# Infini-attention beside an MLP: memory read as two 64-row products, VectorE with at most one SBUF operand, and another job order

## The chip, the cores and the metric

The kernel runs on one core of a Trainium2 chip. A core has TensorE (PE in the profile; its weight loads are PEld), VectorE (DVE), ScalarE (ACT), GpSimd (POOL) and SyncE (SP, which here issues most DMAs). SBUF is the working memory of 128 partitions; PSUM has eight banks of 128 x 512 f32, into which TensorE writes. The metric is device time in microseconds; before the change it is 690.04, the median of 3 runs (689.83 to 690.31).

## What is computed

x has 2048 rows of 512. It is normalised, then two branches are added to it:

```python
x = A_x
xn = _layernorm(x, axis=-1)
return x + _A_ref(xn, A_wq, A_wk, A_wv, A_wo, A_beta) + _B_ref(xn, B_w1, B_b1, B_w2, B_b2)
```

Branch B is an MLP of width 1792 with its own layer norm and GELU. Branch A is attention with 32 heads of 16 in four segments of 512 rows, with a compressed memory M, z carried from segment to segment:

```python
for s in range(N):
    qs, ks, vs = q[:, :, s], k[:, :, s], v[:, :, s]
    logits = jnp.einsum("bhqd,bhkd->bhqk", qs, ks) * scale + mask
    p = _softmax(logits, axis=-1)
    a_dot = jnp.einsum("bhqk,bhkd->bhqd", p, vs)
    pq = phi(qs)                      # where(t > 0, t + 1, exp(t))
    num = jnp.einsum("bhld,bhde->bhle", pq, M)
    den = jnp.einsum("bhld,bhd->bhl", pq, z)[..., None] + 1e-6
    a_mem = num / den
    o = g * a_mem + (1.0 - g) * a_dot
    pk = phi(ks)
    M = M + jnp.einsum("bhld,bhle->bhde", pk, vs)
    z = z + jnp.einsum("bhld->bhd", pk)
```

## The kernel before

Attention runs in 16 blocks i = 4 s + g: segment s, group g of eight heads (128 partitions of head dimensions). Large products are f16 in three terms: every operand is split into a high and a low half. For a block, `qk_proj` projects q and k into a PSUM bank, ACT writes the high half and, where phi is needed (q from segment 1 on, k up to segment 2), Exp of the bank into SBUF; `qk_low` forms the low half on DVE and sends both through DRAM (kd, qd) into the layout in which the scores are formed (kst, qst). `qk_phi` finishes phi on DVE: a minimum and a product in SBUF (L632), then a maximum of the bank plus that (L634, L638).

`m_job` forms scores a first time (L740) and reduces their masked maximum on DVE (L747); `m_row` turns the maxima to rows, which go through DRAM (md) into two further rows of qst. `s_job` forms the scores transposed with the maximum already subtracted (L782), ACT exponentiates them (L789), POOL clears the upper triangle (`s_mask`), `pv` multiplies with the values (L816, four column quarters of the array), and `o_norm` divides by the sum: Ln and Exp(-) on ACT, one Newton step on DVE (L662, L663), products on POOL.

The memory is read in `a_mem` for blocks 4 to 15. `z_cols` lays M and z out with zeros between heads (mx, on DVE). Four products of 128 rows give, for 128 tokens each, numerators and denominators with tokens on partitions (L681, two banks); DVE forms the reciprocal and the quotient (rd, L684 to L689, into rc); `a_turn` transposes it back with four transposes (L696) and ACT copies it to ame (L698), which `o_norm` adds on POOL.

The MLP is `d_job` (hidden tiles, L586 on w1s), `gelu` and `h_split` on ACT and POOL, and `e_jobs` (L931); `out_jobs` is the output projection (L951). Weights are scaled by powers of two from sums of squares: `w_trace` takes sums on TensorE with a reduction on DVE (L384), `w_scale` adds them over partitions with a product with ones (L414).

The order is written out: `ORDER` names, character by character, the stream from which the next job comes, and `BANKS` the PSUM bank of every `dense()`. Each engine takes its instructions in that order. A bank is written again when its readers are done. SP takes its DMAs in the same order.

Of the kernel before, what the change touches and what calls it, by code (L numbers as in the profile page):

```python
# [19 lines left out]
P = 128  # L20
# [5 lines left out]
H = 32  # L26
# [33 lines left out]
def streams():  # L60
# [78 lines left out]
    "auhhwhhhlkhhkhhbth6xc6khldlhhie$hfhhhhkjhx6f78$hhahhv$rg7%%8%k8%h8bR8cs8mRde8i&ff9m9gj9n&!n&#y&z((CA)9*(CD+(+2"  # L139
    "BBDo)(X*+X,)-,*(()X!*3oXX,9,XXYFZFF0Py1F.zpF,-o!FR4F#.Z-0FB9,.14BR4QFZF041/XZA,X/01/-/.4F$=4/=p:4E4P24#F2;F:=="  # L140
    "44:4G4GFGX=GF<XHGFF3>4HaI>::IHI>IFGqGb3Xc?X2GH;GFyFFdzG@XHf>XF:EHYCX<X?DiQZ0IIA>;IB1I>GJG<3KGXCLBe:XGG;ZHD@MPX"
    "4HNFFIIHQIO0IFFG1Z4f4<GGX?0@41GHHqFZFy0FGY>F4a[1?4zXjAFHFZIIIIb4@0B4414Z[[FEcJ4KXXd4440[1eBXfGGGZ4LXXFMG440G]F"
    "1FH4fUN4ZP^H0X1YFFFyH4OFFIIIZiAIGzF044444GFGCF]GGX4_ETX1H]H4Q]HIIIDIGJGKBGZH4LPVX0BaXy1ZzG0GFMC4X1H4AZ4^FID0H_"
    "NOIITIFG4XGFUG4H4G1GFHBH4XFFIIIIFFJYFKURR4B4FLFMbFZNFRXOE0S4W4GcFGeX4144HGGGRF5HFIIHQIIdFFGSZG5FHFPyG0GGXzSFH1"
    "Z2VHASIIQIEI0GJGKLGXC13BX2DPfUXTGMGW444fNZV44H0HHjIIIOQIBFFG41a4bGGX4iHGGF3Y44H4HFFF4yFZ5FI01IIzBZAI0F1JZFX04X"
    "C4K1DZ404FjXX1B44X4EXX4YT4Z44LFG2cG4M44eGFiFd01X43H4FGGZN0HXXFF5IHIIOIGFGXXGGF2XWFG1FZfHf0XPVHFU4441Z01YZyE44H"
    "a3zIIIQIGGJ44UK4L4C4AGGMTG4D4N4WH4bPHHOIIIIGGGXB0BVXGGFyFF1HzHHBFIcIdAIZIRCFFFe01RDXFJKFFXZi0RLMXXFWTN41fR4fE4"
    "GZGGB4440XHOG1FGH4SHFFFIIYIQISGGa5FVZ4X4GG0UFXP4HH2FG1Z0FbyH4FzFIQIIAI1S5XSPBFZJ4X03KLCc1EZDM4GiGT5NOG4XBXGGj4"
    "H4W0HH4IQIII1GGF444FGG4VXGFFyHHHFFFIYIII24dZ4e440F13zFZ0FJ4XC4D1Z0XXFEfXK41BTABXL4Z4XM44041GGGPX44UGFFH44HNU4f"
    "4OFYZGF04WXV44XH1F2ZFIIIIFGFy53G0zFFXX1XGHZGG44FHC440TXXXIED1QYI2HZI0IGG41JKH4BZjj44GGGH34L4UBMX4HWNXX0OIIIIFF"  # L150
    "G4144FZG0FyF1ZGH0zFXXGF1G4Z4XFH0FFHYIIIIVCUBFRJ4KREDL1M4WNT4ORGBGGS5Z240GFHFS4FF1GRFF5HHFIZIIIGG0y1FFF4zHSVF4C"
    "4Z40GGG4HDE44HSIITIIG5G1J44XXK4ZLGGBMBGHXXXNXH4HFI3I2IOI0GGHF3441WVyzGFG4XGFFHCY4FFF444HXIZT0I1Z20IB1DIFFJ4ZXX"
    "04KX1BFLZX40E1X4XY4ZM0NF1FZG4444GF5UG4XH0414GGFXH4FFHIIZOI2IGFF440X1GGFHXZ40G1GHF34HXFXXYEIIZII01ZJW444KGG44LV"
    "GG34GMHH4H444IINOI0IGG1HG44G4GZ4W440HH41IIII4Z04JKL1444M444N4O44SSSS5555"
# [4 lines left out]
    "01234567012345670123460123647013654701542670546173250641732570641257106457106457103645120365412306524306512430"  # L159
    "65713062451372046130472610342561037425036714023674012743610273406217306723146723156042713560421630541263045126"  # L160
    "30452630451263745126345126347152630471526045271352671532467135246357021463570214635721426357426357421063574210"
    "63547231506472361507236175236415273641503641752034172053724105637120357612035712036571203471206514270651427034"
# [22 lines left out]
def infini_mixer_kernel(ctx: ExitStack, tc: tile.TileContext, x, wq, wk, wv, wo, beta, w1, b1, w2, b2, out):  # L185
# [278 lines left out]
    nws = {}  # L464

    mhalf = cst.tile([P, 4], F32, name="mhalf")
    G.memset(mhalf, -0.5)

    def norm_sums(h, tiles):

# [582 lines left out]
```

## Time and profile before

| | us |
|---|---|
| median of 3 runs | 690.04 |
| the profiled execution's span | 690.7 |
| PE busy | 680.1 |
| DVE busy | 498.9 |
| ACT busy | 471.4 |
| POOL busy | 346.4 |
| mask reduction on DVE, L747 | 234.0 |
| score exponentials on ACT, L789 | 204.2 |
| memory products on PE, L681 | 13.4 |
| their transposes on PE, L696 | 7.3 |

The page gives no time for the profiled execution beside its span, 690.7 us. Matmuls are pipelined, so busy times of PE overlap: a row's length covers more than its share of the array, and the distance of starts tells the rate. "Idle before" is the time an engine stood still before the instructions of a group, with what ended it.

### The profile page before, as it was taken

Reading aid. Unit: us, or ns where it says so; the run is one execution under the profiler, and the core shown is the slowest. Engines: PE = TensorE matmul, PEld = TensorE weight load, DVE = VectorE, ACT = ScalarE, POOL = GpSimd, SP = SyncE. Lnnn points to the kernel's source line nnn. Section 1 sums busy time; section 2 is a strip of 40 time slices with the busy share of each in tenths; the row PEclk is TensorE's granted clock in tenths of the full one; section 3 lists DMA queues with packets and bytes.
Section 4 is the critical chain, followed back from the end, with each engine's and each line's share of the span. In section 5 each row is a group of like instructions: output and inputs, shape, how many; then the busy total and the mean of one; then the engine's idle time right before and its main releaser. Section 6 shows DMA issues by size and latency. Waiting matters only on the chain.

```text
span 690.7 us, 15732 instructions
## 1 busy us (share of the span) xinstructions
PE 680.1 (98%) x5787; PEld 394.6 (57%) x5787; DVE 498.9 (72%) x1613; ACT 471.4 (68%) x877; POOL 346.4 (50%) x574
## 2 busy tenths in 40 slices
PE   8999999999999999999999999999999999999997
PEld 6764565656644565665555555566565446565543
DVE  5789888986796669676695875878468565787622
ACT  4578898897765578578836838556956554777960
POOL 5576587663525444373545344534372425365652
PEclk9999999999999999999999999999999999999999
DMA  9788433203320342312222133231411222420101
GB/s 267 230 199 218 113 91 105 79 2 91 81 49 16 87 108 55 95 47 72 70 70 57 31 79 86 57 85 39 99 35 56 69 65 61 107 65 2 33 1 61
DMA packets 52889, 55.83 MB, mean 81 GB/s; under 512 B 4990, under 2 KB 41868, under 8 KB 52812
## 3 DMA queue, kind: packets, MB, share of 16 engines
q1 hardware_dynamic: 50508, 50.64, 26.8%
q0 software_dynamic: 2304, 4.20, 3.8%
q8 instruction: 45, 0.74, 0.5%
q14 instruction: 32, 0.26, 0.1%
HBM read 37.77 MB, written 17.05 MB: 79 GB/s over the span
## 4 chain that ended last, share of the span: by engine, by line
PE 87%; DVE 8%; DMA 2%; issue 1%; SPq 1%; POOL 1%; ACT 0%; DVEq 0%
PE dense L586 35%; PE dense L931 20%; PE dense L816 10%; PE dense L951 6%; PE dense L782 6%; PE dense L740 5%; DVE dense L747 4%; PE dense L681 2%; PE dense L696 1%; DVE mc L747 1%; PE dense L564 1%; DMA pt<-in_A_wv_dram 1%; PE dense L651 1%; DMA qst<-md 1%; PE dense L382 0%
## 5 line engine op out<-in xcount | busy, mean ns | idle before, releaser
L747 DVE CUSTOM_DVE_ANT_0 dense<-dense,mask 128x384 f32<-128x384 f32 (+3 forms) x512 | 234.0, 528 | 33.9 <-PE dense L740 33.6
L789 ACT ACTIVATE pt<-dense,qkcs 128x512 f32<-128x512 f32 (+1 forms) x384 | 204.2, 628 | 46.3 <-PE dense L782 46.2
L931 PE MATMUL dense<-w2s,hT 128*128 128x512 f16 x672 | 166.3, 380 | 0.2 <-DVE hT L884 0.2
L586 PE MATMUL dense<-xnT,w1s 128*128 128x256 f16 x1344 | 160.2, 273 | 0.3 <-DVE mc L747 0.3
L803 POOL TENSOR_SCALAR_AFFINE_SELECT pt<-pt 128x256 f32<-128x256 f32 x256 | 99.4, 422 | 108.2 <-ACT pt L789 107.8
L586 PEld LDWEIGHTS <-w1s 128*128 128x128 f16 x1344 | 129.6, 98 | 29.1 <-issue 6.2
L905 POOL TENSOR_TENSOR hT<-hh,hT 128x512 f16<-128x512 f32 x64 | 67.6, 1057 | 83.6 <-ACT hT L903 70.4
L931 PEld LDWEIGHTS <-hT 128*128 128x128 f16 x672 | 61.3, 98 | 68.6 <-issue 13.4
L816 PE MATMUL dense<-pt,vt 128*32 128x512 f32 (+3 forms) x1024 | 78.0, 436 | 0.0
L747 DVE DVE_READ_ACCUMULATOR2_ANT mc<- 128x1 f32 x512 | 74.2, 145 | 0.0
L884 DVE SCALAR_TENSOR_TENSOR hT<-dense,sc,cb 128x512 f32<-128x512 f32 x64 | 43.5, 680 | 33.8 <-PE dense L586 25.2
L847 POOL TENSOR_TENSOR nN<-nN,oT 128x512 f32<-128x512 f32 x16 | 20.9, 1308 | 73.9 <-DVE oT L663 73.9
L901 POOL TENSOR_SCALAR hh<-hT,sc 128x512 f32<-128x512 f32 x64 | 42.5, 664 | 24.1 <-ACT hT L891 15.5
L816 PEld LDWEIGHTS dense<-pt,vt 128*32 128x32 f32 x1024 | 31.1, 109 | 40.7 <-issue 29.4
L782 PE MATMUL dense<-qst,kst 50*128 50x384 f16 (+3 forms) x512 | 52.1, 299 | 1.8 <-DMA qst<-md 1.8
L740 PE MATMUL dense<-kst,qst 48*128 48x384 f16 (+3 forms) x512 | 52.2, 298 | 0.0
L891 ACT ACTIVATE hT<-hT,b1t 128x256 f32<-128x256 f32 x112 | 47.0, 496 | 5.0 <-DVE hT L884 4.6
L903 ACT ACTIVATE hT<-hh 128x512 f16<-128x512 f32 x64 | 37.3, 583 | 14.9 <-POOL hh L901 14.9
L951 PE MATMUL dense<-wos,oT 128*128 128x512 f16 (+2 forms) x204 | 44.0, 367 | 0.8 <-DVE acc L953 0.7
L586 PE MATMUL dense<-xnT,wks 128*128 128x512 f16 (+1 forms) x252 | 44.5, 329 | 0.2 <-DVE mc L747 0.2
L586 PE MATMUL dense<-xnT,wqs 128*128 128x512 f16 (+1 forms) x252 | 44.2, 329 | 0.1
L586 PE MATMUL dense<-wvs,xnT 128*128 128x512 f16 x192 | 43.9, 379 | 0.1
(227 smaller groups left out, 832.0 us busy)
## 6 DMA issues: line engine op xcount, KB each, us to landing
kst<-kd SPq DMA_DIRECT2D x32, 192.0 KB
qst<-qd SPq DMA_DIRECT2D x32, 192.0 KB
qd<-hl SPq DMA_DIRECT2D x36, 128.0 KB
kd<-hl SPq DMA_DIRECT2D x33, 128.0 KB
acc<-in_A_x_dram SPq DMA_DIRECT2D x16, 256.0 KB
acc<-in_B_b_dram POOLq DMA_DIRECT2D x16, 256.0 KB, 4.2
out_dram<-acc SPq DMA_DIRECT2D x15, 256.0 KB
xt<-in_A_x_dram SPq DMA_DIRECT2D x14, 256.0 KB
```

The source lines that it names most:

```text
L586: T.matmul(p, ws(k, a), xs(k, b), start=i == 0, stop=i == 3 * KT - 1)
L740: T.matmul(p[:, o:o + n], stk[i, 0][r, t, P * qb:P * qb + P], stk[i, 1][r, t, :n], start=True, stop=True)
L747: V.tensor_tensor_reduce(p[:, o:o + n], p[:, o:o + n], mask[:, 512 - n:], 1.0, -3e38, OP.add, OP.max, mc[i][:, 4 * b + t, qb:qb + 1])
L782: T.matmul(p[:, o:o + n], stk[i, 1][r, t, P * kb:P * kb + P], stk[i, 0][r, t, P * kb:], start=True, stop=True)
L789: A.activation(pt[i, 4 * b + t][:, OFF[kb]:OFF[kb] + n], p[:, c:c + n], AF.Exp, scale=qkcs[:, 1, i % NG:i % NG + 1])
L803: G.affine_select(v, v, pattern=[[0, 2], [1, P]], compare_op=OP.is_ge, fill=0.0, base=0, channel_multiplier=-1)
L816: T.matmul(p[32 * c:32 * c + 32, P * kb:], vt[s, kb][:, 4 * g + c, 16 * odd:16 * odd + 32], pt[i, 2 * c + odd][:, OFF[kb]:OFF[kb] + LEN[kb ...
L884: V.scalar_tensor_tensor(hz[:, f0:f + 1, :], p[:, :256 * n].rearrange("p (f c) -> p f c", f=n), col(CG + fh), cbt[hf].unsqueeze(1).to_broa ...
L891: A.activation(hz[:, f, :], hz[:, f, :], AF.Gelu_apprx_tanh, bias=b1t[:, fo:fo + 1])
L905: G.tensor_tensor(hT[:, z, 1, :], hht[j, c], hT[:, z, 0, :], op=OP.subtract)
L931: T.matmul(p, t[:, u, P * a:P * a + P], w2s[:, fo, v, :], start=fi == 0 and n == 0, stop=fi == FH - 1 and n == 2)
L951: T.matmul(p[:, c], o[:, u, P * b:P * b + P], wos[:, g, v, c], start=i == 0, stop=i == 3 * NG - 1)
```

## The change

Five edits, and a new order.

1. phi: Exp of the projection is now written back into its PSUM bank, and a new step `qk_floor` takes max(x, 0) from the bank into SBUF on DVE; `qk_phi` adds min(exp, 1) from the bank to it. The minimum and product in SBUF (L632 of before) is gone.
2. The Newton step of `o_norm` has its estimate in a PSUM bank (rec), no longer in SBUF (nD).
3. The memory is read with head dimensions on partitions: mx now holds, for each half of 64 partitions, M with the gate in 64 columns and z repeated in 64 columns, and two products of 64 rows each, over 512 tokens, give numerators in partitions 0 to 63 and denominators in 64 to 127 of a bank. Ln and Exp on ACT estimate the reciprocal, `a_share` multiplies on DVE and forms the Newton residue, `a_step` ends both on POOL. The transposes and the copy are gone.
4. mx and the sum of z are formed on POOL.
5. Small constants (gr, one scale, qkcs[:, 0]) go; quad, quadg and tiny come.

```diff
@@ streams
             put(n + "1", ("Tv", i, w))
             if not (s == 0, s == NSEG - 1)[w]:
+                put(n + "1", ("Tu", i, w))
                 put(n + "2", ("Tw", i, w))
...
             put("mem1", ("Q", i))
-            put("mem2", ("Qt", i))
+            put("mem2", ("Y", i))
+            put("mem3", ("Yg", i))
@@ ORDER, first line
-    "auhhwhhhlkhhkhhbth6xc6khldlhhie$hfhhhhkjhx6f78$hhahhv$rg7%%8%k8%h8bR8cs8mRde8i&ff9m9gj9n&!n&#y&z((CA)9*(CD+(+2"
+    "auhhwhhhlkhhkhhbth7xc7khldlhhie%hfhhhhkjhx7f89%hhahhv%rg8&&9&k9&h9bR9cs9mRde9i(ff!m!gj!n(#n($y(zz))CA*!+)CD,),"
@@ plan
-        need = "G" if k == "G" else "E" if k == "S" or k == "O" and key[2] == 1 or k == "T" and (
-            key[1] >= NG if key[2] == 0 else key[1] < NU - NG) else tab
+        need = "G" if k == "G" else "E" if k in ("S", "Q", "Tu") or k == "O" and key[2] == 1 else tab
@@ qk_proj
-        e = None
-        if phi:
-            e = sb.tile([P, 512], F32, name=("phq", "phk")[which])
-            A.activation(e, p, AF.Exp, scale=qkcol(2, 1 - which, g))
-        prj[i, which] = p, hl, e
+        prj[i, which] = p, hl
...
+    def qk_floor(i, which):
+        g = i % NG
+        p = prj[i, which][0]
+        e = pqt[i, which] = sb.tile([P, 512], F32, name=("phq", "phk")[which])
+        c = qkcol(2, 1 - which, g)
+        V.tensor_scalar(e, p, c, 0.0, op0=OP.mult, op1=OP.max)
+        A.activation(p, p, AF.Exp, scale=c)
+
     def qk_phi(i, which):
         s, g = divmod(i, NG)
-        p, _, e = prj[i, which]
-        V.tensor_scalar(e, e, 1.0, qkcol(3, 1 - which, g), op0=OP.min, op1=OP.mult)
+        p, e = prj[i, which][0], pqt[i, which]
         if which == 0:
-            V.scalar_tensor_tensor(e, p, 0.0, e, op0=OP.max, op1=OP.add)
+            V.scalar_tensor_tensor(e, p, 1.0, e, op0=OP.min, op1=OP.add)
...
     def z_cols(i):
-        g = i % NG
-        mx[i] = sm.tile([P, P + GH], F32, name="mx")
-        V.tensor_tensor(mx[i][:, :P].rearrange("p (a b c) -> p a b c", a=4, b=2),
...
-        V.tensor_scalar(mx[i][:, P:], half, zst[:, g:g + 1], None, op0=OP.mult)
+        s, g = divmod(i, NG)
+        if s == 1:
+            G.tensor_scalar(quadg[:, g], quad, bg[:, g, 3:4], 0.0, op0=OP.mult, op1=OP.add)
+        mx[i] = sm.tile([P, P], F32, name="mx")
+        G.tensor_tensor(mx[i][:, :64].rearrange("p (a b c) -> p a b c", a=2, b=2),
...
+        G.tensor_scalar(mx[i][:, 64:].rearrange("p (a b) -> p a b", b=DH), quad.unsqueeze(2).to_broadcast([P, 4, DH]),
+                        zst[:, g:g + 1], 0.0, op0=OP.mult, op1=OP.add)
 
     def a_mem(i):
...
+        q = pqt[i, 0]
+        mp[i] = [dense() for b in range(2)]
+        R = [slice(64 * b, 64 * b + 64) for b in range(2)]
+        for r, p in zip(R, mp[i]):
+            T.matmul(p, mx[i][r, :], q[r, :], start=True, stop=True)
+        for r, p in zip(R, mp[i]):
+            A.activation(q[r, :], p[64:, :], AF.Ln, bias=tiny[:64])
+        A.activation(q, q, AF.Exp, scale=-1.0)
+
+    def a_share(i):
+        q = pqt[i, 0]
+        t = ame[i] = sb.tile([P, 512], F32, name="ame", bufs=2)
+        R = [slice(64 * b, 64 * b + 64) for b in range(2)]
+        for r, p in zip(R, mp[i]):
+            V.tensor_tensor(t[r, :], p[:64, :], q[r, :], op=OP.mult)
+            V.scalar_tensor_tensor(q[r, :], p[64:, :], 1e-6, q[r, :], op0=OP.add, op1=OP.mult)
+
+    def a_step(i):
+        q, t = pqt[i, 0], ame[i]
+        G.tensor_scalar(q, q, 1.0, -2.0, op0=OP.mult, op1=OP.add)
+        G.tensor_tensor(t, t, q, op=OP.mult)
@@ kv
-        V.tensor_tensor(zst[:, g:g + 1], zs[i], zst[:, g:g + 1], op=OP.add)
+        G.tensor_tensor(zst[:, g:g + 1], zs[i], zst[:, g:g + 1], op=OP.add)
@@ o_norm
         elif part == 1:
-            log_recip(nd[i][2], d)
+            rec[i] = dense()
+            A.activation(d, nd[i][2], AF.Ln)
+            A.activation(rec[i], d, AF.Exp, scale=-1.0)
         elif part == 2:
-            newton(nd[i][2], nd[i][2], d)
+            r = nd[i][2]
+            V.tensor_tensor(r, r, rec[i], op=OP.mult)
+            V.scalar_tensor_tensor(r, r, 2.0, rec[i], op0=OP.subtract, op1=OP.mult)
```

Where the order moved is shown at three places. The first is TensorE's queue at the memory products of block 4, the first block that reads the memory; before:

```order
L931 MATMUL dense_2419<-w2s,hT_126 128x512
L651 MATMUL dense_2643<-ident,phk 128x128 x4
L681 MATMUL dense_2652<-mx,phq 128x136 x2
L681 MATMUL dense_2653<-mx,phq 128x136 x2
L586 LDWEIGHTS w1s
L586 MATMUL dense_2664<-xnT,w1s 128x256
```

and now (L811 is `pv`, L777 `s_job`):

```order
L811 MATMUL dense_2612<-pt,vt_89 32x128 x4
L677 MATMUL dense_2632<-phq,mx 128x512
L677 MATMUL dense_2633<-phq,mx 128x512
L777 LDWEIGHTS kst_93
L777 MATMUL dense_2649<-qst_91,kst_93 128x512
L777 LDWEIGHTS kst_93
L777 MATMUL dense_2650<-qst_91,kst_93 128x512
```

The products stood between work in full rows; now they stand between the column quarters of `pv` and the half rows of `s_job`, and no L696 follows later.

The second place is ACT's queue behind the same products. Before, ACT had only the copy of the transposed quotient there:

```order
L707 ACTIVATE vt_86<-dense_3143 128x16x2x16
L903 ACTIVATE hT_126<-hh 128x2x256
L698 ACTIVATE ame<-dense_3191 128x512
L789 ACTIVATE pt<-dense_3203,qkcs 128x512
L789 ACTIVATE pt<-dense_3204,qkcs 128x512
```

and now (L679 and L680 are in `a_mem`, L784 the score exponentials):

```order
L656 ACTIVATE pkn<-dense_2598 128x512
L902 ACTIVATE hT_130<-hh 128x2x256
L679 ACTIVATE phq<-dense_2632,tiny 64x512
L679 ACTIVATE phq<-dense_2633,tiny 64x512
L680 ACTIVATE phq<-phq 128x512
L784 ACTIVATE pt<-dense_2649,qkcs 128x512
L784 ACTIVATE pt<-dense_2650,qkcs 128x512
```

The two Ln and the Exp stand ahead of the exponentials of the scores that TensorE forms right after the memory products.

The third place is DVE's queue in the start, where the sums of W2's first half are reduced (L384 before, L386 now) and the scale is made from the product with ones (L388 to L438 before, L390 to L438 now); before:

```order
L624 SCALAR_TENSOR_TENSOR phq_554<-dense2_468,phq_554 128x512
L448 SCALAR_TENSOR_TENSOR w1s_102<-w1s_102,sc_105 128x512
L384 SCALAR_TENSOR_TENSOR dense5_582,am_104<-dense5_582,ident_74 128x128
L624 SCALAR_TENSOR_TENSOR ame_576<-dense0_563,ame_576 128x512
L388 TENSOR_SCALAR dense6_642<-dense6_642 128x1
L392 TENSOR_SCALAR sc_105<-dense6_642 128x1 x2
L438 SCALAR_TENSOR_TENSOR sc_105<-sc_105 128x1
L884 SCALAR_TENSOR_TENSOR hT0_126<-dense4_628,sc_105,cb_252 128x512
```

and now:

```order
L621 SCALAR_TENSOR_TENSOR phq_554<-dense2_467,phq_554 128x512
L448 SCALAR_TENSOR_TENSOR w1s_104<-w1s_104,sc_107 128x512
L386 SCALAR_TENSOR_TENSOR dense6_581,am_106<-dense6_581,ident_74 128x128
L883 SCALAR_TENSOR_TENSOR hT0_129<-dense4_613,sc_107,cb_256 128x512
L390 TENSOR_SCALAR dense5_641<-dense5_641 128x1
L394 TENSOR_SCALAR sc_107<-dense5_641 128x1 x2
L438 SCALAR_TENSOR_TENSOR sc_107<-sc_107 128x1
```

The reading of the first two hidden tiles (L884 before, L883 now) has moved ahead of the scale: on TensorE both hidden tiles (L586 before) now stand ahead of the product with ones (L414), where only one did.

More of the change, by code (lines that the diff above doesn't have):

```diff
@@ L144 @@
[L144 to L148, printed above, removed]
@@ L304, in w_load @@
             else:
-                stage["1"] = [sb.tile([P, 512], F32, name=t)
-                               for t in ("rc", "ame")]
+                stage["1"] = [sb.tile([P, 512], F32, name="ame", bufs=2) for t in range(2)]
             for j in range(2):
```

116 lines of the change are left out of this document (46 added, 70 removed).

## The prediction

> **What bounds the kernel now.** First the head of the page, its chain and two of its groups; then one table of windows: start, middle, tail.
>
> ```profile
> span 690.7 us, 15732 instructions
> PE 680.1 (98%) x5787; PEld 394.6 (57%) x5787; DVE 498.9 (72%) x1613; ACT 471.4 (68%) x877; POOL 346.4 (50%) x574
> PE 87%; DVE 8%; DMA 2%; issue 1%; SPq 1%; POOL 1%; ACT 0%; DVEq 0%
> L847 POOL TENSOR_TENSOR nN<-nN,oT 128x512 f32<-128x512 f32 x16 | 20.9, 1308 | 73.9 <-DVE oT L663 73.9
> L901 POOL TENSOR_SCALAR hh<-hT,sc 128x512 f32<-128x512 f32 x64 | 42.5, 664 | 24.1 <-ACT hT L891 15.5
> ```
> ```profile
> 0.00:80.00 80.00, 74.51 (x628) 48.93 (x629) 63.21 (x223) 53.49 (x101) 49.78 (x81) 1.00 0.80 219
> 80.00:660.00 580.00, 579.32 (x5006) 333.70 (x5004) 426.83 (x1377) 408.13 (x759) 286.78 (x478) 1.00 0.26 64
> 660.00:690.70 30.70, 26.23 (x158) 11.93 (x156) 8.91 (x14) 9.82 (x19) 9.79 (x16) 0.98 0.10 35
> ```
>
> In the windows the columns are the stretch, its length, then PE, PEld, DVE, ACT and POOL busy, granted clock, DMA share, GB/s. TensorE covers 579.32 of the 580 us between 80 and 660 at clock 1.00, while DVE is busy 74%, ACT 70% and POOL 49% of that stretch. A busy share alone could hide stalls between pipelined matmuls, so I look at starts: in the timeline a row's length runs over the next row's start, and the distance of starts is what counts.
>
> ```profile
> 169.37 1.09 PE L681 MATMUL dense<-mx,phq 128*128 128x136 f32 x8
> 170.30 1.26 PE L586 MATMUL dense<-xnT,w1s 128*128 128x256 f16 x10
> ...
> 210.26 0.81 PE L931 MATMUL dense<-w2s,hT 128*128 128x512 f16 x3
> 210.91 0.60 PE L696 MATMUL dense<-ident,rc 128*128 128x128 f32 x4
> 211.35 0.81 PE L931 MATMUL dense<-w2s,hT 128*128 128x512 f16 x3
> 212.09 0.39 PE L782 MATMUL dense<-qst,kst 50*128 50x512 f16 x2
> 212.32 0.38 PE L740 MATMUL dense<-kst,qst 48*128 48x384 f16 x4
> 212.54 0.38 PE L782 MATMUL dense<-qst,kst 50*128 50x384 f16 x4
> 212.85 0.83 PE L586 MATMUL dense<-xnT,w1s 128*128 128x256 f16 x6
> ```
>
> Three L931 products start at 210.26 and the next row at 210.91: 0.65 us, 0.217 each, no room between them. So in the middle TensorE's own work sets the time, and a microsecond taken off it there is a microsecond off the end. The chain's 8% of DVE is mostly the mask reduction (L747) freeing a bank just as TensorE wants it; TensorE's idle time in all of the middle is 580 - 579.32 = 0.7 us, so that share is no store of gain. In the first 80 us TensorE idles 5.5 us, and there waits do count.
>
> **The change, part by part.** *Memory read on TensorE.* It happens for blocks 4 to 15, twelve times. Removed: four products 128x136 (each recorded as two, x8): 170.30 - 169.37 = 0.93 us; and the four transposes: 211.35 - 210.91 = 0.44. Together 12 x 1.37 = 16.4 us. Added: two f32 products of 512 columns that use 64 rows each. A recorded f32 product costs 0.93 / (8 x 136) = 0.855 ns a column, so 512 columns cost 0.438, and the two records of a product 0.875. Side by side the two row halves cost 0.875 a block, one behind the other 1.75. Rows for side by side: the two L782 products of 512 columns (half the rows each) take 212.32 - 212.09 = 0.23 us for both, against 0.217 for one L931. That is f16; for f32 the nearest row is L816, whose products use quarters of the columns:
>
> ```profile
> 76.63 2.29 PE dense L816 x32
> ```
>
> Its 32 records cover 2 x 4 x 1280 = 10240 columns, which one behind another would be 8.75 us and took 2.29 (a row of the chain, in order of time). I take 0.875: added 12 x 0.875 = 10.5 us. Net -5.9 us; with the other end (1.75) it would be +4.6.
>
> *Changes of the array's division.* From L931 to L782 it takes 212.09 - 211.35 = 0.74 for three products of 0.217, so 0.09 us goes to the change; from L782 back to L586 the four records (1024 half-row columns, 0.22 us side by side) take 0.31, again 0.09. Counted along TensorE's order, there are 266 places before where work in full rows, half rows or quarter columns follows another kind, and 276 after, since the new products are half-row work and often stand between full-row work. +10 x 0.1 = +1.0 us. The Trainium skill, TensorEngine Tiling (Array Packing), Key Properties, says that a change of tiling mode drains the array; the trace agrees with its 0.09 us. Without that rule the new products would look 1.0 us cheaper than I count them.
>
> *A wait in the start.* In the chain, in order of time, and in TensorE's timeline:
>
> ```profile
> 30.66 1.31 DVE phk L632
> ...
> 32.70 1.03 DVE wqs L448
> 33.73 0.60 DVE phq L624
> 34.33 0.96 DVE w1s L448
> 35.29 0.28 DVE dense L384 x2
> ```
> ```profile
> 33.14 1.47 PE L586 MATMUL dense<-xnT,w1s 128*128 128x256 f16 x12
> 35.61 0.38 PE L414 MATMUL dense<-am,ones 128*128 128x1 f32 x2 [1.00 <-DVE dense L384]
> ```
>
> TensorE waits 1.00 us at 35.6 for a queue of DVE work. The new order puts the next hidden tile ahead of that L414: 12 products of 256 columns, half of 0.217 each, 1.3 us of work where it stood idle. L632, which took 1.31 us in the queue, becomes a read of PSUM besides. The wait goes: -1.0 us (between 0, if DVE's queue is late by as much again, and -1.2). No DMA is issued by the moved tile. What is late next is the second wait of the start, and it stays:
>
> ```profile
> 62.72 2.63 DMA md<-mhl
> 65.67 3.85 DMA qst<-md
> 67.84 0.39 PE L782 MATMUL dense<-qst,kst 50*128 50x512 f16 x1 [0.41 <-DMA qst<-md]
> 69.57 0.39 PE L782 MATMUL dense<-qst,kst 50*128 50x512 f16 x1 [1.35 <-DMA qst<-md]
> ```
>
> Between the row transpose of block 0 and its first score product there stand the same seven L931 groups before and after, and one more maximum job after (0.2 us); on SP's queue the same transfers lie between md and qst. So 1.76 us of waiting for these two DMAs stays within 0.3, and I count 0. On SP the loads of kst and qst for block 0 now stand ahead of an acc load and of W1's second half; no wait of TensorE on them is in these rows, and I count 0 for that too.
>
> *DVE, ACT, POOL.* Prices:
>
> ```profile
> 0.00:690.70 690.70, 16.04 (x24) 1.00 0.31 81
> ...
> 0.00:690.70 690.70, 21.99 (x72) 1.00 0.31 81
> ...
> L632 DVE TENSOR_SCALAR phk<-phk,qksc x12: 450/558/1384, 30.6 to 452.2; 128x512 f32<-128x512 f32 x12
> L638 DVE SCALAR_TENSOR_TENSOR phk<-dense,phk 128x512 f32<-128x512 f32 x12 | 8.3, 692 | 0.4
> L829 DVE SCALAR_TENSOR_TENSOR nN<-dense,bg,nN 128x512 f32<-128x512 f32 x16 | 12.0, 750 | 9.5 <-PE dense L816 9.2 <-POOL hT L905 0.3
> L698 ACT ACTIVATE ame<-dense 128x512 f32<-128x512 f32 x12 | 7.5, 622 | 11.6 <-POOL nN L849 7.6 <-PE dense L696 3.9
> L618 ACT ACTIVATE phk<-dense,qksc 128x512 f32<-128x512 f32 x12 | 8.2, 682 | 0.0
> ```
>
> The first two rows are windows of L632 alone and of the instructions on rd alone (L684 to L689). DVE loses these 16.0 and 22.0 us and the two small products for mx. It gains 24 floors from PSUM (between 0.69, L638, and 0.75, L829 with a column as scalar; I take 0.75: 18.0) and 48 half-height operations (between 0.35, if rows counted, and 0.69; I take 0.69 as in L638: 33.1). That is at most +13 us on 498.9, less what mx took; the refinement of the reciprocal keeps its columns and reads PSUM with one operand. ACT gains 36 operations of 0.62 and loses 12: +15 us on 471.4. Exp into PSUM has no row; between 0.62 and 0.75 for the same columns, I take L618's 0.68, no change. POOL gains 12 x (0.66 + 1.31) = 24 us for the last step (L901 and L847 for the prices) and two small products a block for mx, at most as much again, on 346.4. All this lies beside TensorE's saturated middle: ACT has 172 us free there, DVE 153, POOL 293. If that cover were gone, it would cost what the wait at the bank costs (the second rival).
>
> Sum in the profiled execution: 690.7 - 5.9 + 1.0 - 1.0 = 684.8. The profile's span is 0.6 above the runs' median (690.04), so for the runs -5.9 gives **684.1 us**.
>
> **Rivals.** *One: DVE and POOL were in each other's way, and that cost TensorE more.* L632 takes 450 ns at the least and 1384 at the most for one shape, so something stops it; 16.04 against 24 x 0.45 = 10.8 is 5.2 us of stalls. The Trainium skill, SBUF — State Buffer, Who interferes with whom, has it that a DVE instruction with two SBUF inputs, or in a two-port mode, excludes a GpSimd instruction that reads SBUF for its whole length, and that one with at most one SBUF input does not. The spread of L632 fits that. If the waits of the start are made of such stalls, more of the 5.5 us idle there goes: up to 4 us beyond the 1.0 counted, 680. Against it: 1.76 of them end on a DMA and more lies before the first weights have landed. It gives 680 to 681.
>
> *Two: the banks are held too long, and TensorE waits.* Before, the two memory products' banks were free after six DVE operations (22.0 / 12 = 1.8 us). Now ACT reads them first (two Ln, one Exp: 1.9 us) and then DVE four times (2.8): 4.7 us, plus what stands ahead on ACT. In TensorE's new order 32 to 124 products stand between a memory product and the next writer of its first bank, 32 x 0.11 to 32 x 0.217, 3.5 to 7 us, at the shortest. If four score exponentials of L618's 0.68 stood ahead of the Ln each time, the chain would be 7.4 us and the shortest cases would lose up to 4 us. From 0.5 us a block (5.9 / 12) the gain is gone; at 0.8 us a block the run ends at 690.0 - 5.9 + 9.6 = 693.7, slower. For it: ACT and DVE both grow. Against it: in the one such block shown, the Ln stand ahead of the score exponentials on ACT, and the middle waits 0.7 us in 580 on the same eight banks.
>
> *Three: the two halves do not run side by side*, so the change does not do what it says. Then -16.4 + 21.0 + 1.0 - 1.0 = +4.6: 694.6. Against it speak the L782 and L816 rows.
>
> **How the numbers follow.** Forecast (681.5 to 687.5) 0.63; rival one 0.10; rival two 0.21, of which 0.08 ends at 687.5 to 688.6, 0.06 within 0.2% of before (688.7 to 691.4; about what a measurement of this kernel can tell from no change) and 0.07 above; rival three 0.06. Faster: 0.63 + 0.10 + 0.08 = 0.81; same 0.06; slower 0.13. The range 679.5 to 690.0 takes in the forecast, rival one and the half of rival two that only eats the gain, and leaves out about 0.15.
>
> **What would show it.** Right: L681 and L696 gone, the two new products of a block starting within 10 ns of each other and 0.9 us to the next row; TensorE's busy sum about 6 us lower, its middle still idle under 2 us; no wait at 35.6; the wait for qst at 68 still there. Wrong: starts of the two halves 0.4 us or more apart (rival three); idle time before L777, L735 or L588 ended by DVE L688 or ACT L680 (rival two); idle in the first 80 us under 2 us (rival one). DVE's floors should show one duration, near 0.7, where L632 spread threefold.

## The result and the profile after

The changed kernel takes 683.88 us, the median of 4 runs (683.47 to 688.27), against 690.17 for the kernel before, measured with it (689.83 to 690.50, 4 runs): a ratio of 0.9917, 95% interval 0.990 to 0.9934. A second set of 6 runs gave 683.33 (682.39 to 688.87), ratio 0.9918 (0.989 to 0.9946). Over both sets eight of the ten executions lie at 682.39 to 684.13 and two apart from them, at 688.27 and 688.87. The profile that came with the result is that of the one at 688.27.

The head of its page, its chain, and the windows as they were shown of before (the stretch, its length, PE, PEld, DVE, ACT and POOL busy, granted clock, DMA share, GB/s):

```profile
span 686.6 us, 15552 instructions
PE 675.4 (98%) x5691; PEld 381.1 (56%) x5691; DVE 508.4 (74%) x1552; ACT 491.0 (72%) x900; POOL 376.9 (55%) x635
PE 89%; DVE 4%; ACT 3%; issue 1%; SPq 1%; DMA 1%; POOL 1%; POOLq 0%; ACTq 0%; DVEq 0%
```
```profile
0.00:80.00 80.00, 73.02 (x586) 47.86 (x590) 64.51 (x211) 50.88 (x96) 48.08 (x80) 0.98 0.81 222
80.00:660.00 580.00, 579.80 (x4975) 322.97 (x4968) 434.92 (x1329) 434.51 (x794) 318.69 (x542) 1.00 0.25 64
660.00:686.60 26.60, 22.53 (x136) 10.32 (x134) 8.98 (x14) 5.66 (x12) 10.12 (x14) 0.99 0.11 40
```

DVE, ACT and POOL all do more than before, and TensorE's middle is as full as it was: 0.2 us idle in 580. The gain in TensorE's sum is there. But in the first 80 us TensorE idles 7.0 us where it idled 5.5, and a granted clock of 0.98 stands in that row. The second profile, of an execution at 683.1 us, shows how the other eight look:

```profile
span 681.4 us, 15552 instructions
PE 673.1 (99%) x5691; PEld 380.0 (56%) x5691; DVE 504.0 (74%) x1552; ACT 491.0 (72%) x900; POOL 376.7 (55%) x635
```
```profile
0.00:80.00 80.00, 75.98 (x646) 50.31 (x647) 65.25 (x228) 55.90 (x106) 49.75 (x83) 1.00 0.80 222
80.00:660.00 580.00, 579.82 (x4958) 321.45 (x4956) 431.02 (x1313) 432.81 (x792) 320.56 (x546) 1.00 0.25 64
```

Here TensorE idles 4.0 us in the first 80. So between the two profiles (spans 686.6 and 681.4) there is one event of about 5 us, of which 3.0 us is idle time of TensorE in the first 80. These are DVE's row and POOL's timeline at the place, first of the profile at 688.27, then of the one at 683.1:

```profile
43.42 5.26 DVE L448 SCALAR_TENSOR_TENSOR w2s<-w2s,sc 128x512 f16<-128x512 f32 x1
...
43.23 1.09 POOL L912 DMA_DIRECT2D acc<-in_B_b_dram  x1 [1.49 <-DMA acc<-in_A_x_dram]
44.02 1.49 POOL L454 TENSOR_TENSOR w2s<-w2s 128x512 f16<-128x512 f32 x1
45.16 1.01 POOL L450 TENSOR_SCALAR w2s<-w2s,sc 128x512 f32<-128x512 f32 x1
45.83 0.99 POOL L900 TENSOR_SCALAR hh<-hT,sc 128x512 f32<-128x512 f32 x1
46.50 0.98 POOL L450 TENSOR_SCALAR pt<-pt,qksc 128x512 f32<-128x512 f32 x1
47.17 0.96 POOL L450 TENSOR_SCALAR w2s<-w2s,sc 128x512 f32<-128x512 f32 x1
```
```profile
43.59 0.75 DVE L448 SCALAR_TENSOR_TENSOR w2s<-w2s,sc 128x512 f16<-128x512 f32 x1
...
43.58 1.09 POOL L912 DMA_DIRECT2D acc<-in_B_b_dram  x1 [1.68 <-DMA acc<-in_A_x_dram]
44.38 1.49 POOL L454 TENSOR_TENSOR w2s<-w2s 128x512 f16<-128x512 f32 x1
```

It is the low part of a piece of W2 (`w_split`), which reads two tensors from SBUF; the change did not touch it. The same operation takes 0.75 us or 5.26, and in the second case it ends at 48.68, 0.55 us after the last of POOL's five operations, so it ran its own length only when that row was through or nearly so. In that profile's chain, in order of time, the price is plain:

```profile
43.42 0.75 DVE w2s L448
44.17 4.43 issue
48.61 0.47 DVE hT L883
49.08 0.60 DVE dense L742
```

The chain knows nothing that DVE waited for and calls 4.43 us "issue". Behind it stands the queue of DVE (hidden tile, eight mask reductions), and TensorE runs dry: between 40 and 60 us it waits 3.6 us, all of it for that queue.

### The profile page after: what moved, and what is told of

It is laid out like the page before. It is cut to its first block, busy times and chain, and to the rows that moved or that the text cites. A ratio compares the mean times of both kernels' runs of the same rounds, so it can differ in the third digit from the quotient of the medians.

```text
span 686.6 us, 15552 instructions
## 1 busy us (share of the span) xinstructions
PE 675.4 (98%) x5691; PEld 381.1 (56%) x5691; DVE 508.4 (74%) x1552; ACT 491.0 (72%) x900; POOL 376.9 (55%) x635
## 4 chain that ended last, share of the span: by engine, by line
PE 89%; DVE 4%; ACT 3%; issue 1%; SPq 1%; DMA 1%; POOL 1%; POOLq 0%; ACTq 0%; DVEq 0%
PE dense L588 36%; PE dense L930 21%; PE dense L811 10%; PE dense L950 6%; PE dense L735 6%; PE dense L777 6%; PE dense L677 2%; DVE dense L742 1%; PE dense L566 1%; DMA pt<-in_A_wv_dram 1%; PE dense L654 1%; DVE w2s L448 1%; PE dense L712 1%; PE dense L384 0%; ACT hT L890 0%
## 5 line engine op out<-in xcount | busy, mean ns | idle before, releaser
L784 ACT ACTIVATE pt<-dense,qkcs 128x512 f32<-128x512 f32 (+1 forms) x384 | 205.0, 625 | 43.3 <-PE dense L777 42.7
L930 PE MATMUL dense<-w2s,hT 128*128 128x512 f16 x672 | 162.4, 380 | 0.0
L811 PE MATMUL dense<-pt,vt 128*32 128x512 f32 (+3 forms) x1024 | 77.7, 436 | 0.2 <-ACT pt L784 0.2
L883 DVE SCALAR_TENSOR_TENSOR hT<-dense,sc,cb 128x512 f32<-128x512 f32 x64 | 43.3, 680 | 33.4 <-PE dense L588 32.9
L735 PE MATMUL dense<-kst,qst 48*128 48x384 f16 (+3 forms) x512 | 54.1, 299 | 0.7 <-DVE mc L742 0.7
L811 PEld LDWEIGHTS dense<-pt,vt 128*32 128x32 f32 x1024 | 30.9, 109 | 41.6 <-issue 27.8
L777 PE MATMUL dense<-qst,kst 50*128 50x384 f16 (+3 forms) x512 | 53.7, 298 | 0.2 <-DVE mc L742 0.2
L902 ACT ACTIVATE hT<-hh 128x512 f16<-128x512 f32 x64 | 37.0, 579 | 12.1 <-POOL hh L900 11.9
L934 DVE SCALAR_TENSOR_TENSOR acc<-dense,sc,acc 128x512 f32<-128x512 f32 x32 | 23.9, 748 | 20.1 <-PE dense L930 19.8
```

Source lines behind the costliest of these rows:

```text
L735: T.matmul(p[:, o:o + n], stk[i, 0][r, t, P * qb:P * qb + P], stk[i, 1][r, t, :n], start=True, stop=True)
L777: T.matmul(p[:, o:o + n], stk[i, 1][r, t, P * kb:P * kb + P], stk[i, 0][r, t, P * kb:], start=True, stop=True)
L784: A.activation(pt[i, 4 * b + t][:, OFF[kb]:OFF[kb] + n], p[:, c:c + n], AF.Exp, scale=qkcs[:, i % NG:i % NG + 1])
L811: T.matmul(p[32 * c:32 * c + 32, P * kb:], vt[s, kb][:, 4 * g + c, 16 * odd:16 * odd + 32], pt[i, 2 * c + odd][:, OFF[kb]:OFF[kb] + LEN[kb ...
L883: V.scalar_tensor_tensor(hz[:, f0:f + 1, :], p[:, :256 * n].rearrange("p (f c) -> p f c", f=n), col(CG + fh), cbt[hf].unsqueeze(1).to_broa ...
L930: T.matmul(p, t[:, u, P * a:P * a + P], w2s[:, fo, v, :], start=fi == 0 and n == 0, stop=fi == FH - 1 and n == 2)
```

## The experiments

**The race at 43 us: the changed kernel again.** No edit.

> The changed kernel once more, for a second profile of it. Theory A (the gain is TensorE work, and the loss in the first 60 us of the first profile is an event of single executions): undisturbed executions at 683.5 to 684.1 us; a profile of about 682 us span, with no DVE operation of w_split near 43 us above 2 us, TensorE's first 80 us busy at least 75 us. Theory B (the stall at 43 us belongs to the program): the same DVE row of about 5 us stands in this profile too, and the profiled execution is at 687 to 689 us.

Measured: 683.33 us, the profile shown above. Theory A: the stall is not in this execution, and one of the six runs is at 688.87.

**Its DVE operation a little later.** The ACT operation that releases it is done in two halves.

```diff
-            A.activation(h, r, AF.Copy, scale=s)
+            for q in ((slice(0, 256), slice(256, 512)) if (m, n) == ("2a", 3) else (slice(0, 512),)):
+                A.activation(h[:, q], r[:, q], AF.Copy, scale=s)
```

> The changed kernel with one ACT operation in two halves: the high part whose end starts the DVE operation that took 5.26 us at 43.4 us in one profile and 0.75 at 43.6 in the other. Two ACT operations of 256 columns take about 0.5 each where one of 512 takes 0.72, so the DVE operation starts some 0.25 us later, surely behind the start of the GpSimd row (43.23 and 43.58 in the two profiles, where the DVE operation came 0.19 and 0.01 us after it). Race theory: now it loses in every execution: all of them 687 to 690 us and a DVE operation of about 5 us in the profile. If the executions near 688 have another cause: 683 to 684.5 us in most executions, as before.

Measured: 687.83 us, 683.36 to 688.85: seven of nine executions at 687.08 or above, two at 683.36 and 683.76, where the unchanged kernel has two of ten near 688. "Every execution" was too much: the profiled one is one of the two, so no profile shows one of the seven. In it the GpSimd row started late, its load having landed late, and the DVE operation 0.05 us after it:

```profile
44.22 0.75 DVE L449 SCALAR_TENSOR_TENSOR w2s<-w2s,sc 128x512 f16<-128x512 f32 x1 [0.31 <-ACT w2s L448]
...
44.17 1.09 POOL L913 DMA_DIRECT2D acc<-in_B_b_dram  x1 [1.82 <-DMA acc<-in_A_x_dram]
```

All profiles in the new order in which this DVE operation stands at the GpSimd row, by how long after the row's first instruction (the DMA issue) it starts; the last one is of the old code in the new order, an experiment further down:

| profile | DVE after the row's start, us | duration, us |
|---|---|---|
| old reciprocal | -0.08 | 0.75 |
| changed kernel, second | 0.01 | 0.75 |
| full rows | 0.03 | 0.75 |
| old phi | 0.05 | 0.75 |
| high part in halves | 0.05 | 0.75 |
| old phi and old reciprocal | 0.14 | 5.33 |
| changed kernel, first | 0.19 | 5.26 |
| old code, new order | 0.67 | 2.82 |

That, with two in ten turned to seven in nine by a delay, makes the race the cause of the executions near 688. No profile shows a start between 0.05 and 0.14, so where exactly it turns is open. The last profile shows how it ends: there the third of the five operations starts 1.01 us after the second (45.03, 46.04) where the row back to back has 0.67, and the DVE operation ends at 46.58, its own 0.75 us after 45.83. It got in at a gap, with three operations of the row still to come.

**The row of GpSimd operations taken apart.** One job moves in `ORDER`: the first addition of b2, five GpSimd operations later.

```diff
@@ GpSimd's instructions
-L912 DMA acc<-in_B_b_dram 128x512
 L454 TENSOR_TENSOR w2s<-w2s 128x512
...
 L450 TENSOR_SCALAR w2s<-w2s,sc 128x512
+L912 DMA acc<-in_B_b_dram 128x512
```

> The changed kernel with the first addition of b2 (a DMA that GpSimd issues, and for which it waits 1.5 to 1.7 us on the load of acc) five GpSimd operations later, behind the row that it holds up. The row then starts as its operations come due and is not piled up behind 43.2 us. Race theory: the low part of W2 at 43.5 us does not meet a row of five operations back to back; all executions 682 to 684.5 us. The operation may still meet a single GpSimd operation and grow by up to 1.5 us; then 684 to 685.5.

Measured: 683.95 us, 683.64 to 684.22 in 4 runs, ratio 0.9905 (0.9892 to 0.9919). The operation took 0.78 us, and the row has gaps again:

```profile
43.99 1.13 POOL L450 TENSOR_SCALAR w2s<-w2s,sc 128x512 f32<-128x512 f32 x1
46.06 0.69 POOL L900 TENSOR_SCALAR hh<-hT,sc 128x512 f32<-128x512 f32 x1 [0.94 <-ACT hT L890]
```

As expected. At two in ten, four runs without the event are no proof that it cannot come; the profile without the pile is the better witness. Against the eight undisturbed executions it is no faster.

**The DVE operation behind the row.** The same low part four jobs later, behind the maxima of block 0; a stream of its own lets `ORDER` place it there.

```diff
-                put("ws%d" % k + m, ("ws", m, c, k))
+                put("ws%d" % (3 if (m, c) == ("2a", 3) else k) + m, ("ws", m, c, k))
```

> The changed kernel with one low part of W2 (the DVE operation at 43.4 us, 5.26 us long in the first profile and 0.75 in the second) put four jobs later, behind the maxima of block 0; nothing else moves on any engine but its ACT partner. Theory A (a race of that operation with a row of GpSimd operations that starts within 0.2 us of it, and what it holds up costs TensorE 4.5 to 5.5 us): every execution between 682 and 684.5 us, none near 688, and no DVE operation above 2 us in the profile. Theory B (the executions near 688 have another cause): one execution in five near 688 still, DVE's long operation or not.

Measured: 684.96 us, 684.09 to 685.99. None near 688, as theory A has it, but from 684.09 up, at and above the upper end of the undisturbed ones (684.13), and four of the five above the 684.5 that it allowed: TensorE's wait moved to another place (0.74 us on the mask reductions before a product of `kv` at 54.55 us). The version above is the better cure.

**The memory read alone.** The changed kernel, in its own order, with phi's minimum taken in SBUF again (one tensor read there, one written) and the reciprocal's refinement reading two tensors from SBUF again. The core:

```diff
     def qk_floor(i, which):
-        V.tensor_scalar(e, p, c, 0.0, op0=OP.mult, op1=OP.max)
-        A.activation(p, p, AF.Exp, scale=c)
+        A.activation(e, p, AF.Exp, scale=c)
     def qk_phi(i, which):
+        V.tensor_scalar(e, e, 1.0, qkcol(3, 1 - which, g), op0=OP.min, op1=OP.mult)
...
-            A.activation(rec[i], d, AF.Exp, scale=-1.0)
+            A.activation(d, d, AF.Exp, scale=-1.0)
```

> The changed kernel in its own order with the old phi and the old reciprocal: the minimum with 1 and the refinement read their two tensors from SBUF again (Exp and the estimate are written to SBUF). TensorE work theory: the same TensorE work, so 683.5 to 684.5 us, the DVE stalls being beside other work. Port theory (the rival in which DVE and POOL in each other's way cost TensorE time): 685 to 688 us, the difference as TensorE idle time ended by DVE or POOL.

Measured: 689.09 us, 686.25 to 693.49 in 12 runs; ratio to before 0.9993 (0.9971 to 1.0015). TensorE's work is the changed kernel's, and in the median hardly anything of the gain is left; between the fastest executions 3.1 us are (686.25 against 689.34). That speaks for the port theory, though the median lies above its range: executions with the event at 43 us, the profiled one among them, are in it. Its profile (the 5.33 of the table; span 689.1) shows in the middle, and in DVE's group of the minimum (shortest, median, longest in ns):

```profile
80.00:660.00 580.00, 577.37 (x4943) 321.69 (x4935) 436.13 (x1326) 430.57 (x787) 321.20 (x537) 1.00 0.25 64
```
```profile
L639 DVE TENSOR_SCALAR phk<-phk,qksc x12: 465/663/1461, 31.3 to 449.4; 128x512 f32<-128x512 f32 x12
```

TensorE idles 2.6 us there where the changed kernel idles 0.2, and the event at 43 us comes on top. In the changed kernel the floor that takes this operation's place has one duration:

```profile
L631 DVE TENSOR_SCALAR phk<-dense,qksc x12: 697/743/758, 29.5 to 445.6; 128x512 f32<-128x512 f32 x12
```

**Each of the two edits alone put back.** The same diff, its first two parts and its last part.

> The changed kernel in its own order with the old phi alone (Exp and the minimum in SBUF, as the experiment that put back both had it); the reciprocal's refinement reads its estimate from PSUM as in the change. Both edits together were worth 3 us without the stall at 43 us (686.3 against 683.3) and more with it. If phi carries them: 686 to 687.5 undisturbed, with stalls of the minimum up to 1.4 us at 137 and 156 us and TensorE idle there. If the refinement carries them: 683.3 to 684.5.

> The changed kernel in its own order with the old reciprocal alone (its estimate in SBUF, both refinement operations with two SBUF operands); phi as in the change. If phi carries the 3 us: 683.3 to 684.3 us. If the refinement carries them: 685.5 to 687, with TensorE waiting behind operations on oT above 0.9 us.

Measured: old phi 685.38 us (684.62 to 686.06), old reciprocal 685.30 (683.87 to 691.43, 12 runs). Old phi costs a steady 2 us against 683.33, a little under what was expected if it carried all; its middle idles 1.9 us (0.2 in the changed kernel). The old reciprocal costs about as much in the median but scatters over 7.5 us; its profiled execution lost time before 20 us too, so how much of that is its own stays open. Neither carries the whole. How a stall comes through is seen in old phi, in DVE's, POOL's and TensorE's timelines:

```profile
132.29 1.39 DVE L639 TENSOR_SCALAR phk<-phk,qksc 128x512 f32<-128x512 f32 x1
133.72 0.69 DVE L645 SCALAR_TENSOR_TENSOR phk<-dense,phk 128x512 f32<-128x512 f32 x1
134.33 0.75 DVE L886 SCALAR_TENSOR_TENSOR hT<-dense,sc,cb 128x512 f32<-128x512 f32 x1
...
132.25 1.16 POOL L907 TENSOR_TENSOR hT<-hh,hT 128x512 f16<-128x512 f32 x1 [0.17 <-ACT hT L905]
...
134.47 0.32 PE L780 MATMUL dense<-qst,kst 50*128 50x384 f16 x1 [0.29 <-DVE phk L645]
135.13 0.38 PE L780 MATMUL dense<-qst,kst 50*128 50x384 f16 x3 [0.34 <-DVE hT L886]
154.26 2.75 PE L933 MATMUL dense<-w2s,hT 128*128 128x512 f16 x12 [1.19 <-DVE phk L645]
```

POOL starts at 132.25, DVE 0.04 later: 1.39 us in place of 0.47 to 0.48, and the two operations behind it free TensorE's banks late. Of the delay some 0.9 is the stall; the rest, as the order of the instructions suggests, is that the minimum now stands between Exp and the sum, where the floor stood ahead of it. No run takes the two apart. The last line is a second such place, behind a minimum of 1.47 us.

**Phi alone, in the order of before.** The floor is taken in place in PSUM, so the order need hardly change: five low parts move ahead of their phi.

```diff
-        V.tensor_scalar(e, e, 1.0, qkcol(3, 1 - which, g), op0=OP.min, op1=OP.mult)
+        V.tensor_scalar(p, p, qkcol(2, 1 - which, g), 0.0, op0=OP.mult, op1=OP.max)
         if which == 0:
-            V.scalar_tensor_tensor(e, p, 0.0, e, op0=OP.max, op1=OP.add)
+            V.scalar_tensor_tensor(e, e, 1.0, p, op0=OP.min, op1=OP.add)
```

> The kernel before with one part of the change alone and in its own order: the floor of phi is taken in place in PSUM and the minimum with 1 reads one tensor from SBUF and one from PSUM, so the 24 operations of old line 632 no longer read and write SBUF at the doubled rate. Five low parts move ahead of their phi; nothing else moves, TensorE's work is the same. My prediction's theory (these stalls lie beside TensorE's saturated middle in this order): 689.5 to 690.5 us. Port theory (their stalls cost TensorE time, as they do in the changed kernel's order where the memory read alone gave 686.3 to 693.5): 686 to 688.5 us. In both, the stalls at that line are gone from the trace.

Measured: 689.60 us against 690.32, 688.55 to 694.16 in 12 runs, ratio 0.9997 (0.9982 to 1.0011): no gain that can be told. The stalls at the line are gone (718 to 757 ns for all 24), and yet the middle is as it was. In the start the 1.00 us wait at 35.6 is gone; TensorE's window from 20 to 40 us, of before's second profile and of this one:

```profile
20.00:40.00 20.00, 18.99 (x182) 15.42 (x181) 15.17 (x43) 11.89 (x23) 12.93 (x20) 1.00 0.72 209
```
```profile
20.00:40.00 20.00, 20.00 (x194) 16.52 (x192) 15.18 (x44) 13.20 (x25) 14.84 (x20) 1.00 0.76 216
```

**The kernel before again.** No edit.

> The kernel before once more, for a second profile. The first profile's span of 690.7 us is about what its runs show as their whole time, though every run whose span is listed is 1.7 us longer than that span; so I expect this profile's span near 688.2 us, TensorE busy the same 680.1 within 1, and its idle time 2 us less than in the first profile, mostly before 80 us. DVE operations that read two tensors from SBUF (or one at the doubled rate) should show stalls of 8 to 12 us in all again, at other instances than before. If they show at the same instances with the same lengths, they are set by the program and not by a race of two engines.

Measured: 690.48 us; the profiled execution at 690.24 with a span of 688.5, as expected. TensorE is busy 678.6, 1.5 less for the same work (within 1 was expected), and its idle time is only 0.7 less (9.9 against 10.6; 2 was expected), because a load at the start is waited for longer (1.2 us in place of 0.4). The waits for qst<-md near 68 us are not in it; from one profile to the other the times of the same instructions part by less than 0.1 us near 30 us and by 2.2 near 160, and these waits, 1.8 us, are most of that. The stalls of DVE stand at the same instances with nearly the same lengths (line 632, the three longest: 1384, 1293 and 1577 ns in the first profile, 1383, 1299 and 1580 in the second; the prediction took 1384 for the longest, which holds for phk alone): in this order, as far as two profiles tell, the two engines meet the same way each time.

**The memory products over all 128 rows.** Each half's rows of mx are zero for the other half.

```diff
-        for r, p in zip(R, mp[i]):
-            T.matmul(p, mx[i][r, :], q[r, :], start=True, stop=True)
+        for h, p in enumerate(mp[i]):
+            T.matmul(p, mx[i][:, h, :], q, start=True, stop=True)
```

> The changed kernel with the memory product of each half over all 128 rows (the other half's rows of mx are zero), so the two products of a block run one behind the other; POOL gets two more small operations a block, and four of its products for mx are placed behind the block before's product. If the halves run side by side in the changed kernel and TensorE's time is the bound: +12 x 0.875 = 10.5, and 16 more changes of the array's division at 0.1, +1.6: 683.4 + 12.1 = 695.5 us, 693.5 to 697, with the second product of a block starting about 0.87 us behind the first. If TensorE had room there, or the halves ran one behind the other already: 683 to 686 us.

Measured: 695.65 us (694.81 to 699.83): 12.3 more than 683.33, expected 12.1. In TensorE's timeline, a block of the changed kernel and the same block of this one:

```profile
170.15 1.13 PE L677 MATMUL dense<-phq,mx 64*128 64x512 f32 x4
171.11 0.60 PE L777 MATMUL dense<-qst,kst 50*128 50x512 f16 x6
```
```profile
165.29 1.98 PE L681 MATMUL dense<-phq,mxz 128*128 128x512 f32 x4
167.21 0.61 PE L781 MATMUL dense<-qst,kst 50*128 50x512 f16 x6
```

0.96 us to the next row against 1.92. How close the halves start is seen in a window of 10 ns, 170.15 to 170.16, in the changed kernel:

```profile
170.15 0.70 PE L677 MATMUL dense<-phq,mx 64*128 64x512 f32 x2
```

Two records are already under way in it; in this experiment a window of 100 ns at the start (165.25 to 165.35) has one. The halves run side by side, and what TensorE does longer is paid in full at the end.

**Old code in the new order, new code in the old order.** Orders of the one kernel were carried over to the other's steps, with banks given to the one longest released.

```diff
@@ old code, order of the changed kernel
-            put("mem2", ("Y", i))
-            put("mem3", ("Yg", i))
+            put("mem2", ("Qt", i))
@@ new code, order of the kernel before
+                put(n + "1", ("Tu", i, w))
...
-            put("mem2", ("Qt", i))
+            put("mem2", ("Y", i))
+            put("mem3", ("Yg", i))
```

> The old memory read, phi and reciprocal in the job order of the changed kernel (the four transposes of a block follow where the new order has the share, or, ten times, behind the previous block's last sum, since there is one tile for their result). TensorE work theory: the products and transposes that the change removed come back (+16.4 us), the new ones go (-10.5), and the changes of the array's division go from 276 to 298 (+2.2 at 0.1): 683.9 + 8.1 = 692.0 us, 690.5 to 693.5. Order theory (the searched order made the gain): 684 to 686.

> The new memory read, phi and reciprocal in the job order of before (the floor and the Exp right behind the low part, the share eight jobs behind the memory product, banks given to the one that was released longest ago). TensorE work theory: as the changed kernel but for 285 changes of the array's division in place of 276, +0.9: 684.8 us, 683.5 to 686.5; more only by waits that this untuned placing adds, which must then show as idle time of TensorE in the windows. Order theory: 689 us or more, with TensorE as busy as in the changed kernel and the difference idle.

Measured: 724.85 us (expected 692.0) and 780.50 (expected 684.8). Both expectations missed by far, and neither theory is told apart by them: an order that is not made for the steps, with banks given out by that rule, costs 33 and 96 us. In the second not all of that is idle time, as was expected: TensorE's busy sum rose too, to 713.2 us from 673.1, with the granted clock at 0.96 in the middle. The second, TensorE's middle and two of its waits (us in all, times, longest):

```profile
80.00:660.00 580.00, 529.72 (x4258) 286.03 (x4253) 379.40 (x1152) 365.51 (x669) 264.92 (x459) 0.96 0.23 58
```
```profile
PE dense L735 <- DVE phq L688: 3.1, 3, 1.3
PE dense L777 <- DVE phq L688: 2.5, 2, 1.8
```

50 us idle, of which these two waits are 5.6. They are those of rival two, banks of the memory products held too long; they are real where the share comes eight jobs behind the product in an order that leaves no room for it.

## Why the prediction was right, and where it was not

684.1 was forecast, 683.88 and 683.33 were measured. The likeliest case came true, and its mechanism, less work on TensorE, made most of the gain: from before's second profile to the changed kernel's second the span fell by 7.1 us, TensorE's busy sum by 5.5 and its idle time by 1.6 (9.9 to 8.3). The 5.5 is near the 4.9 worked out from the rows (-5.9 + 1.0), and the memory read over all 128 rows bears out the price. How much of it the order brought by itself is not measured: the two runs that crossed code and order have busy sums of 691.5 and 713.2 us, so an order moves that sum too. One step failed, one condition was not seen, and that the total is so close is in part luck: the forecast had 1.0 us from one wait, of which 0.2 came, and what made up for it were idle time in the middle (0.5 us less), in the tail (0.4 less) and at a load in the start (0.6 less), for which no gain was counted. By its steps:

- **The memory read on TensorE, -5.9.** Right. The halves run side by side, 0.96 us to the next row with a change of the array's division in it. Undoing that alone costs what two products of 0.875 and the added changes of the array's division come to (12.3 measured, 12.1 worked out), so the price of a column, the price of a change (0.1) and the one-to-one passage to the end hold together for work that is added; the price of a change was not tried by itself. That work taken off comes out at the end as well hangs on a condition, told under rival one. TensorE's busy sum fell by 4.7 us between the first profiles and by 678.6 - 673.1 = 5.5 between the second, where -5.9 and +1.0 make -4.9; two profiles of the kernel before differ by 1.5.
- **The wait at 35.6, -1.0.** This step failed. The reason given was right in one half: the wait was made by DVE's queue with the 1.38 us of L632 in it, and without that stall it goes, in the old order too (before_phi). But another wait stands in its place, 0.77 us for POOL's split of the moved tile's own weights. It comes less from the order than from the change of phi: ACT's Exp now waits for the floor on DVE, and ACT's queue hands the delay on to the split. ACT, POOL and TensorE in the changed kernel, then ACT and TensorE in the experiment with old phi, which has the same order and no floor:

```profile
30.27 0.66 ACT L632 ACTIVATE dense<-dense,qksc 128x512 f32<-128x512 f32 x1 [2.63 <-DVE phk L631]
32.66 1.16 POOL L454 TENSOR_TENSOR w1s<-w1s 128x512 f16<-128x512 f32 x1 [4.05 <-ACT w1s L452]
33.87 2.58 PE L588 MATMUL dense<-xnT,w1s 128*128 128x256 f16 x22 [0.77 <-POOL w1s L454]
```
```profile
30.09 0.69 ACT L634 ACTIVATE phk<-dense,qksc 128x512 f32<-128x512 f32 x1 [1.97 <-DVE hl L624]
33.19 3.08 PE L591 MATMUL dense<-xnT,w1s 128*128 128x256 f16 x24
```

Without the floor Exp waits 0.66 us less, and the 24 products of the tiles take 2.93 us to the next row (36.12) with no wait of their own shown, where they take 3.57 in the changed kernel (two at 32.72, the rest, then the next row at 36.29). The prediction priced the floor on DVE and took Exp into PSUM as no change on ACT; that Exp must now wait for the floor was not in it.

- **The wait for qst at 68 stays.** It did not, but it was not in the kernel's other profile either: it belonged to one execution. That profile's run was also further from the median than the prediction took it to be: every run of this kernel whose span is listed lies 1.7 us above it (runs of other versions up to 2.2), so a span of 690.7 is a run near 692.4, not 690.0. The forecast took differences, so its sum does not suffer.
- **DVE, ACT and POOL hidden, 0.** Right for the changed kernel: between the second profiles DVE grew by 5.7 us, ACT by 19.5 (15 was counted; the Ln over 64 rows takes 0.685 us where 0.62 was taken, which is 1.6 of the difference), POOL by 28.8, and TensorE's middle stayed at 0.2 us idle.
- **Rival one, DVE and POOL in each other's way.** It was taken as something that could add up to 4 us of gain to the start. The experiments show it in another shape. In the old order, taking phi's stalls away is worth nothing that can be told. In the new order, leaving both edits out costs 686.25 - 682.39 = 3.9 us between the fastest executions and 5.8 between the medians. The memory read without them keeps 3.1 us of gain between the fastest executions and none that can be told in the median (ratio 0.9993, 0.9971 to 1.0015). So the two halves of the change are not a sum of -5.9 and 0: in this order the whole gain needs both. How much of the cost is stalls, and how much the minimum's place between Exp and the sum, was not taken apart; and whether an order made for the memory read alone would keep the gain was not tried.
- **Rival two** is not in the changed kernel, as the 0.2 us show; **rival three** is refuted by full_rows.

What was missing altogether is the race at 43 us. It costs about 5 us in two executions of ten. It is rival one's mechanism at a place where the change left two SBUF operands, and nothing in before's one profile showed it: the longest L448 there took 1.58 us.

## What to carry to other kernels

Where TensorE is full, time its work by the distance of starts, and a microsecond off it is a microsecond off the end, but only as long as the other engines' delays stay covered: phi's old form cost 2 us in the new order, and nothing that could be told in the old one. When a step is put ahead of another, ask which engine now waits for it, not only what it costs on its own. Take two profiles of the same kernel before charging a wait in its start to the kernel. Where executions fall into two groups, look for an operation of one engine with two durations, and at what the other engines began just before.

## What the runs showed of the hardware

A DVE operation with two operands in SBUF can be held up not by one GpSimd instruction but by a whole row of them: 5.26 us in place of 0.75, over a DMA issue and five operations back to back. The Trainium skill, SBUF — State Buffer, Who interferes with whom, has it that a DVE instruction with two SBUF inputs contends with a GpSimd instruction that reads SBUF, and that the order of issue, not the shape of the operation, decides who blocks. The runs agree on who wins (0.05 us behind the start of the row the DVE operation still passes, 0.14 behind it does not), and show beyond it that the operation was not let in between GpSimd's instructions while they came back to back, and was where they left a gap. In the first profile it started 0.60 us before the first of the five operations (43.42 against 44.02) and did not get through all the same; what the DMA issue ahead of them does to it the traces do not show.

TensorE's granted clock fell in the first profile, to a mean of 0.95 between 40 and 60 us and 0.97 between 60 and 80. In windows of 4 us it is 1.00 from 40 to 56, while the waits come, then 0.73 and 0.85, then 1.00 again. The stall alone does not make that: with a stall as long (5.33) and nearly as much idle time, the memory read alone keeps 1.00. Why the clock fell in the one execution stays open. The changed kernel's first profile, then that of the memory read alone:

```profile
40.00:60.00 20.00, 16.40 (x133) 8.79 (x132) 19.87 (x50) 13.78 (x25) 11.07 (x13) 0.95 0.78 208
60.00:80.00 20.00, 19.82 (x141) 10.71 (x143) 18.23 (x79) 17.61 (x36) 14.84 (x22) 0.97 0.83 212
```
```profile
40.00:60.00 20.00, 16.75 (x137) 8.81 (x134) 19.87 (x54) 15.00 (x27) 12.67 (x15) 1.00 0.79 215
60.00:80.00 20.00, 18.99 (x148) 9.88 (x151) 18.60 (x75) 16.90 (x36) 14.57 (x23) 1.00 0.72 197
```
